# Attention and token/channel mixer on one core: 32 bytes of filler moved, channel part put in another order

## The chip, the cores and the metric

The kernel runs on one core of a Trainium2 chip, as one program. The metric is the device time of the program in microseconds (us). The kernel before was timed in three runs: 935.6, 936.44 and 939.02 us, median 936.44 us.

## What is computed

The reference is a decayed attention whose output goes through a token-mixing and a channel-mixing network, all in fp32:

```python
def _attn_ref(q, k, v, f):                      # 8 x 8 heads x 576 x 64
    ...
    scores = scale * np.matmul(q, k.transpose(0, 1, 3, 2))
    cum = np.cumsum(np.log(np.clip(f, 0.0001, 1.0)), axis=-1)
    decay = cum[:, :, :, None] - cum[:, :, None, :]
    ...                                         # causal mask, softmax
    return np.matmul(attn, v)

def _moe_ref(x, w_tok1, w_tok2, w_ch1, w_ch2):  # x: 8 x 576 x 512
    xt = x.transpose(0, 2, 1)
    h = np.maximum(xt @ w_tok1, 0.0) @ w_tok2
    u = x + h.transpose(0, 2, 1)
    h2 = np.maximum(u @ w_ch1, 0.0) @ w_ch2     # 512 -> 1536 -> 512
    return u + h2
```

This case is about the last two lines, the channel part: `h2` and the sum that leaves.

## The kernel before

All tokens of the 8 batches stand in one row of 4608. The attention and the token part run batch by batch (32 pairs of heads), and write `u` to DRAM (`ud`). The channel part then goes over the 4608 tokens in five chunks (`WIDE`): three of 2 x 512 tokens and two of 2 x 384. Both matrix products of a chunk are done by a seven-product (Strassen-like) scheme on 2 x 2 blocks. Every fp32 operand is split into a high and a low part, so that one product is three matmuls: high weights by high data, low by high, high by low (lines L1047, L1048, L1049 for the first matrix in `uprod`, L1128, L1129, L1130 for the second in `mul`, reached through `product`).

The weights of one such group (two blocks, high and low, 2 KB in each partition, 256 KB in all) are loaded by one DMA into a buffer `wq` (L962, in `weights`) and used by six matmuls. There are nine `wq` buffers. `wq0` to `wq4` are allocated early, in the pool `mix`. `wq5` to `wq8` come later: at the end of the attention `swap(0)` closes the right-hand pool that held the attention's inputs and opens a new one in its place, with 24 buffers `H` (the hidden rows), six `tmp` and those four `wq`. Pools on the right-hand side grow down from the top of SBUF. The last tile of the old right-hand pool was a filler of 32 bytes, `even0`, which went with that pool.

Around the matmuls, in the second product of a chunk, ScalarE writes the high part of a hidden row into one of six `st` buffers (L489), and VectorE the low part (L498, or L501 with the relu). In the first product VectorE and ScalarE gather the seven partial products from PSUM into `tmp` and `H` (L983, L1059, L1073, L1076, L1082, L1087), and combine rows (L975, L977). At the end of a chunk, `rest_in` loads `u` again into a quarter of an `xt` buffer (L1145), `join` adds a finished partial sum (L1156), `leave` adds the accumulator in PSUM (L1167) and sends the result out (L1171). In the last chunk the last product is ordered differently (`fin`): all 18 matmuls for the first half of the output's channels, then 18 for the second, and `leave` then works on two parts of 192 tokens each.

The order of all work on every engine is a table of numbers, `ORDER`, one row for each of PE, DVE, ACT, POOL and SP (the DMA queue); each number is an operation in the order in which `build` writes them. `Plan.run` takes these orders as they are and gives out buffers by them. All DMAs of the channel part are issued by SP, in order.

Of the kernel before, what the change touches and what calls it, by code (L numbers as in the profile page):

```python
# [9 lines left out]
F32 = mybir.dt.float32  # L10
# [5 lines left out]
P = 128  # L16
# [1344 lines left out]
def attn_mixer_kernel(  # L1361
# [101 lines left out]
    for kind, shape, dt in (  # L1463
# [6 lines left out]
        ("xn", [P, 2, 1024], F32R),  # L1470
    ):
        tiles(ap[kind in ATT[1]], kind, shape, dt, n_(kind))
    ap[0].tile([P, 8], F32, name="even0")

    E["H"], E["tmp"], E["st"] = {}, {}, {}

# [59 lines left out]
```

## Time and profile before

| | us |
|---|---|
| median of three runs | 936.44 |
| the profiled execution | 936.74 |
| its span, from first to last instruction | 935.0 |
| TensorE (PE) busy in the span | 912.3 (98%) |
| VectorE (DVE) busy | 712.9 (76%) |
| ScalarE (ACT) busy | 520.7 (56%) |
| GpSimd (POOL) busy | 237.3 (25%) |
| DMA queue q1, share of 16 engines | 84.3% |

A busy time on PE covers the whole stay of a matmul in the pipeline, and matmuls overlap, so it doesn't tell at what pace they follow each other; that is read from their starts in the timeline. The first matmul of the channel part starts 391.76 us into the span, between the last pieces of the attention, and from 410 us on PE does nothing else. Its matmuls are 512 wide up to 726.80 us, and 384 wide from there on, with some groups of 512 still among them up to 778 us.

### The profile page before, as it was taken

What the parts mean: (1) busy time and instruction counts of PE and PEld (TensorE: products, weight loads), DVE (VectorE), ACT (ScalarE), POOL (GpSimd) and SP (SyncE); (2) the same over time, 40 slices, a digit from 0 to 9 for tenths busy, and PEclk for the clock granted to TensorE, in tenths of its full rate; (3) what the DMA queues carried; (4) which work ended last, traced back from release to release, by engine and by line L of the source; (5) the groups of instructions that cost most, each with busy time, mean ns of one, the idle gap of its engine ahead of it and who ended that gap; (6) DMA issues with size and microseconds to landing.
All of it is one profiled execution on the core that took longest, in us unless ns stands there. A gap on an engine that the chain in (4) does not pass through costs nothing.

```text
span 935.0 us, 26743 instructions
## 1 busy us (share of the span) xinstructions
PE 912.3 (98%) x10270; PEld 782.2 (84%) x10270; DVE 712.9 (76%) x1894; ACT 520.7 (56%) x1340; POOL 237.3 (25%) x320
## 2 busy tenths in 40 slices
PE   8999999999999999999999999999999999999996
PEld 5678888788888787888888888888888899999996
DVE  7998888888788868554698547985389845984685
ACT  5989998998789978631364124540245313541251
POOL 4477777676656552100000000000000000000000
PEclk9999999999999999999999999999999999999999
DMA  7898999999899786669887777878788888989885
GB/s 230 269 278 267 314 274 293 300 297 277 266 307 289 244 251 176 178 197 290 276 246 233 226 243 236 268 227 255 212 250 251 275 289 285 293 280 301 281 283 168
DMA packets 143871, 242.49 MB, mean 259 GB/s; under 512 B 15936, under 2 KB 71488, under 8 KB 143744
## 3 DMA queue, kind: packets, MB, share of 16 engines
q1 hardware_dynamic: 143648, 240.64, 84.3%
q8 instruction: 81, 1.33, 0.6%
q14 instruction: 46, 0.38, 0.1%
q10 hardware_dynamic: 96, 0.15, 0.0%
HBM read 199.52 MB, written 41.21 MB: 257 GB/s over the span
## 4 chain that ended last, share of the span: by engine, by line
PE 78%; DVE 7%; DMA 6%; ACT 3%; POOL 2%; issue 2%; SPq 1%; DVEq 0%; ACTq 0%; POOLq 0%
PE bank L1047 9%; PE bank L1049 9%; PE bank L1048 9%; PE bank L1130 9%; PE bank L1128 9%; PE bank L1129 9%; PE bank L1245 7%; PE bank L747 5%; PE bank L891 4%; PE bank L862 3%; DVE pr L788 3%; ACT pr L792 1%; DMA d_raw<-ud 1%; DMA raw<-in_qk 1%; DMA cb<-decd 1%
## 5 line engine op out<-in xcount | busy, mean ns | idle before, releaser
L792 ACT ACTIVATE pr<-pr,nmin 64x64 f32<-64x64 f32 (+4 forms) x320 | 176.7, 559 | 17.7 <-DVE nmin L788 17.3
L489 ACT ACTIVATE st<-H 128x512 fp32r<-128x512 f32 (+1 forms) x210 | 119.5, 586 | 102.7 <-PE bank L1129 75.6
L1128 PE MATMUL bank<-st,wq 128*128 128x512 f32 (+1 forms) x420 | 155.5, 370 | 0.8 <-DMA wq<-wd 0.8
L1130 PE MATMUL bank<-st,wq 128*128 128x512 f32 (+1 forms) x420 | 155.8, 371 | 0.0
L1129 PE MATMUL bank<-st,wq 128*128 128x512 f32 (+1 forms) x420 | 155.1, 369 | 0.0
L747 PE MATMUL bank<-raw 64*64 64x448 f32 (+6 forms) x1408 | 113.0, 407 | 2.6 <-issue 0.8
L788 DVE CUSTOM_DVE_ANT_0 pr<-bank,cb 128x448 f32<-128x448 f32 (+3 forms) x260 | 108.8, 455 | 6.1 <-PE bank L753 3.0
L498 DVE TENSOR_TENSOR st<-H,st 128x512 fp32r<-128x512 f32 (+1 forms) x150 | 92.2, 632 | 14.3 <-ACT st L489 14.1
L891 PE MATMUL bank<-pf,vr 64*64 64x256 f32 (+3 forms) x2048 | 97.7, 314 | 0.8 <-DVE pf L870 0.3
L872 ACT ACTIVATE pf<-bank 128x512 f32<-128x512 f32 x152 | 84.2, 596 | 9.7 <-PE bank L862 5.7
L1128 PEld LDWEIGHTS bank<-st,wq 128*128 128x128 f32 x420 | 78.8, 188 | 11.4 <-ACT st L489 1.1
L1130 PEld LDWEIGHTS bank<-st,wq 128*128 128x128 f32 x420 | 78.8, 188 | 10.7
L1129 PEld LDWEIGHTS bank<-st,wq 128*128 128x128 f32 x420 | 78.9, 188 | 10.6
L983 DVE TENSOR_TENSOR tmp<-bank,tmp 128x512 f32<-128x512 f32 (+1 forms) x80 | 50.3, 633 | 45.0 <-PE bank L1049 38.7
L1059 ACT ACTIVATE tmp<-bank 128x512 f32<-128x512 f32 (+1 forms) x30 | 16.6, 553 | 121.3 <-PE bank L1049 115.7
L891 PEld LDWEIGHTS bank<-pf,vr 64*64 64x64 f32 x2048 | 75.3, 133 | 8.6 <-issue 1.7
L747 PEld LDWEIGHTS bank<-raw 64*64 64x64 f32 x1408 | 53.1, 135 | 29.4 <-issue 11.6
L862 PE MATMUL bank<-ident,pr 64*128 64x64 f32 x1536 | 65.0, 225 | 5.0 <-DVE nmin L788 2.4
L862 PEld LDWEIGHTS bank<-ident,pr 64*128 64x128 f32 x1536 | 58.9, 139 | 10.5 <-issue 4.2
L922 POOL TENSOR_TENSOR xt<-xt,rb 128x64 f32<-128x64 f32 (+1 forms) x64 | 52.5, 841 | 52.3 <-DVE xt L910 19.6
L1073 ACT ACTIVATE H<-bank 128x512 f32<-128x512 f32 (+1 forms) x30 | 16.4, 553 | 85.4 <-PE bank L1049 80.9
L792 ACT ACTIVATION_READ_ACCUMULATOR pr<-pr,nmin 128x1 f32 (+1 forms) x320 | 62.9, 197 | 0.0
(169 smaller groups left out, 2115.8 us busy)
## 6 DMA issues: line engine op xcount, KB each, us to landing
wq<-wd SPq DMA_DIRECT2D x420, 256.0 KB
raw<-in_qk SPq DMA_DIRECT2D x32, 576.0 KB
cb<-decd SPq DMA_DIRECT2D x26, 576.0 KB
d_raw<-in_w_ch SPq DMA_DIRECT2D x48, 256.0 KB
wd<-sg SPq DMA_DIRECT2D x24, 512.0 KB
vr<-in_v SPq DMA_DIRECT2D x64, 160.0 KB
rb<-recd SPq DMA_DIRECT2D x32, 320.0 KB
wd<-sg SPq DMA_DIRECT2D x24, 384.0 KB
```

Of the source, the lines that this page charges most:

```text
L489: nc.scalar.activation(out, in_, func, scale=scale)
L498: nc.vector.tensor_tensor(out, in_, asf(hi), op=ALU.subtract)
L747: nc.tensor.matmul(at(buf)[HALF[h], of : of + n], q[:, i0 : i0 + D], k[:, j0 : j0 + n], start=t not in (0, 1), stop=not nd, skip_group_che ...
L788: nc.vector.tensor_tensor_reduce(o, x, y, -1.0 / D**0.5, c0[:m, NS + z : NS + z + 1] if t == 5 else 3e38, op0=ALU.add, op1=ALU.min, accum_ ...
L792: nc.scalar.activation(x, x, AF.Exp, bias=E["nmin"][sm][:m, t : t + 1], scale=-1.0, accum_out=E["rec"][rm][:m, c : c + 1])
L862: nc.tensor.transpose(at(ps[s])[:, k * D : (k + 1) * D], at(pr)[r, x, :, :].rearrange("p a b -> p (a b)"), E["ident"][r, r])
L872: p.op("ACT", d_act(512), lambda src_=src_, o=o: nc.scalar.activation(o(), src_(), AF.Copy), rd=[ps[s]], wr=[(pt, s)], bufs=[ps[s], pt])
L891: nc.tensor.matmul(at(av[z])[o, 256 - w : 256], at(vr)[r, vblk(j), :], at(pt)[r, c : c + w], start=j == 4, stop=gi == 2, skip_group_check= ...
L1047: nc.tensor.matmul(o, wt[:, 0, :], h_, start=(first and k == 0), stop=False, skip_group_check=True)
L1128: nc.tensor.matmul(o, wt[:, 0, :], h_, start=(first and x == 0), stop=False, skip_group_check=True)
L1129: nc.tensor.matmul(o, wt[:, 1, :], h_, start=False, stop=False, skip_group_check=True)
L1130: nc.tensor.matmul(o, wt[:, 0, :], l_, start=False, stop=(x == FX - 1), skip_group_check=True)
```

## The change

The 32-byte tile `even0` leaves the attention's pool and gets a pool of its own, opened on the right-hand side before the attention's, which stays open to the end. So the filler now stands at the very top of SBUF. The attention's own buffers keep their addresses (the filler stood above them before, as it does now). The buffers that `swap(0)` opens in their place (`H`, `tmp`, `wq5` to `wq8`) now begin 32 bytes lower. In the built program `wq5` lies at byte 221152 of a partition before and at 221120 after, `wq0` at 122560 in both. Divided by 64, the first address leaves 32, the other two leave nothing, and all 34 late buffers go the same way; all other operands of these matmuls (`st`, `ux`, `sg`, `ring`, the old token weights, `wq0` to `wq4`) lie at multiples of 64 in both.

The tables of the order are written anew for the channel part. No instruction is added or removed on any engine. On PE the sequence of operations is the same up to the 54th matmul of the channel part; before that only `wq` slots differ. On SP the first two DMAs that change places are those of the first chunk's `u`.

```diff
@@ -46,25 +46,25 @@
...
-        "2716 2725 2710 2728 2731 2737 2746 2719 2713 2749 2752 2722 2758 2734 2740 2767 2743 2770 2761 2773 2755 2779 "
...
+        "2716 2725 2710 2728 2731 2737 2713 2722 2719 2746 2749 2734 2740 2752 2758 2743 2767 2770 2773 2761 2755 2779 "
...
@@ -1457,6 +1457,8 @@
     tiles(mixp, "ux", [P, max(WIDE)], F32R, n_("ux"))
     E["uh"].update(E["ux"])
     E["wq"] = {(("wq", i),): mixp.tile([P, 2, 2, P], F32R, name=f"wq{i}") for i in range(n_("wq"))}
+    even = ctx.enter_context(tc.tile_pool(name="even", bufs=1, side="right"))
+    even.tile([P, 8], F32, name="even0")
     att = [tc.tile_pool(name=f"att{x}", bufs=1, side=side) for x, side in enumerate(("right", "left"))]
...
         tiles(ap[kind in ATT[1]], kind, shape, dt, n_(kind))
-    ap[0].tile([P, 8], F32, name="even0")
```

The end of the program, in two queues. These are the last instructions of DVE before; the last matmuls of PE write bank3, and bank3 rows of 192 are the two parts of that last result:

```order
L1167 TENSOR_TENSOR xt0_144<-bank5_68,xt0_144 128x384
L1156 TENSOR_TENSOR xt0_144<-xt0_144,tmp2_8166 128x384
L1167 TENSOR_TENSOR xt0_144<-bank0_63,xt0_144 128x192
L1167 TENSOR_TENSOR xt0_144<-bank3_66,xt0_144 128x192
L1167 TENSOR_TENSOR xt1_145<-bank1_64,xt1_145 128x384
L1167 TENSOR_TENSOR xt0_144<-bank0_63,xt0_144 128x192
L1167 TENSOR_TENSOR xt1_145<-bank6_69,xt1_145 128x384
L1167 TENSOR_TENSOR xt0_144<-bank3_66,xt0_144 128x192
```

And the last of DVE in the changed kernel, where the last matmuls write bank3 as well and bank1 holds the half before it:

```order
L1167 TENSOR_TENSOR xt1_145<-bank2_65,xt1_145 128x384
L1156 TENSOR_TENSOR xt1_145<-xt1_145,tmp3_8170 128x384
L1167 TENSOR_TENSOR xt0_144<-bank1_64,xt0_144 128x192 x2
L1167 TENSOR_TENSOR xt1_145<-bank5_68,xt1_145 128x384
L1167 TENSOR_TENSOR xt1_145<-bank3_66,xt1_145 128x192 x2
```

Before, three instructions that don't read bank3 stand between its two parts; now the two parts are the last two.

The end of SP's queue before, from the last load of weights (`wq7`) on:

```order
L962 DMA wq8_8173<-wd2_2_136 128x512
L962 DMA wq7_8172<-wd2_0_134 128x512
L1171 DMA out_t<-xt1_145 128x384 x2
L1145 DMA xt0_144<-ud7_127 128x192
L1171 DMA out_t<-xt0_144 128x192 x4
L1171 DMA out_t<-xt1_145 128x384
L1171 DMA out_t<-xt0_144 128x384
L1171 DMA out_t<-xt1_145 128x384
L1171 DMA out_t<-xt0_144 128x384
```

And the same of the changed kernel:

```order
L962 DMA wq7_8175<-wd2_0_134 128x512
L1145 DMA xt1_145<-ud6_126 128x192
L1171 DMA out_t<-xt1_145 128x384
L1145 DMA xt1_145<-ud7_127 128x192
L1171 DMA out_t<-xt0_144 128x384 x2
L1171 DMA out_t<-xt1_145 128x384
L1171 DMA out_t<-xt0_144 128x192
L1171 DMA out_t<-xt1_145 128x384
L1171 DMA out_t<-xt0_144 128x384
L1171 DMA out_t<-xt0_144 128x192
L1171 DMA out_t<-xt1_145 128x192 x2
```

The four `out_t` of 384 that closed the queue now stand ahead of the two parts of the last result, which are the last two DMAs. The load of `wq7`, the first weights of the last product, is the last load of weights in both, and in both it stands behind the same point of PE's program (it may start once all but the last 54 matmuls are done).

## Rows read from the trace of the kernel before

**Rows 1.** The page, part 1: the span, and busy us (share of span) xinstructions.

```profile
span 935.0 us, 26743 instructions
PE 912.3 (98%) x10270; PEld 782.2 (84%) x10270; DVE 712.9 (76%) x1894; ACT 520.7 (56%) x1340; POOL 237.3 (25%) x320
```

**Rows 2.** Windows: stretch, its us, busy us of each engine, granted clock, DMA.

```profile
391.70:410.00 18.30, 18.24 (x184) 14.99 (x181) 8.61 (x20) 5.31 (x13) 3.32 (x4) 1.00 0.44 139
410.00:560.00 150.00, 150.00 (x654) 122.40 (x653) 101.58 (x167) 47.92 (x84) 0.00 (x0) 1.00 0.83 253
560.00:730.00 170.00, 170.00 (x742) 138.76 (x741) 130.48 (x216) 65.24 (x117) 0.00 (x0) 1.00 0.80 242
751.00:927.90 176.90, 175.99 (x993) 173.41 (x991) 123.26 (x252) 60.59 (x126) 0.00 (x0) 1.00 0.87 277
927.90:935.00 7.10, 0.00 (x0) 0.00 (x0) 1.76 (x5) 0.00 (x0) 0.00 (x0) 0.84 0.44 152
```

**Rows 3.** Waits on PE, 410 to 928 us: us in total, times, longest.

```profile
PEld bank L1128 <- ACT st L489: 1.1, 1, 1.1
PE bank L1128 <- DMA wq<-wd: 0.8, 1, 0.8
```

**Rows 4.** Timeline of PE, 512 wide: starts of eight matmuls (start us, us, what).

```profile
672.90 0.39 PE L1128 MATMUL bank<-st,wq 128*128 128x512 f32 x1
...
679.71 0.39 PE L1047 MATMUL bank<-ring,wq 128*128 128x512 f32 x1
...
701.91 0.39 PE L1128 MATMUL bank<-st,wq 128*128 128x512 f32 x1
...
707.51 0.39 PE L1128 MATMUL bank<-st,wq 128*128 128x512 f32 x1
...
711.60 0.39 PE L1128 MATMUL bank<-st,wq 128*128 128x512 f32 x1
...
714.39 0.39 PE L1128 MATMUL bank<-st,wq 128*128 128x512 f32 x1
...
718.49 0.39 PE L1128 MATMUL bank<-st,wq 128*128 128x512 f32 x1
...
724.08 0.39 PE L1128 MATMUL bank<-st,wq 128*128 128x512 f32 x1
```

**Rows 5.** The same, 384 wide.

```profile
907.71 0.34 PE L1128 MATMUL bank<-st,wq 128*128 128x384 f32 x1
...
910.83 0.35 PE L1128 MATMUL bank<-st,wq 128*128 128x384 f32 x1
...
911.38 0.33 PE L1128 MATMUL bank<-st,wq 128*128 128x384 f32 x1
...
913.98 0.34 PE L1128 MATMUL bank<-st,wq 128*128 128x384 f32 x1
```

**Rows 6.** Timeline of the last 18 us: PE.

```profile
920.07 0.34 PE L1130 MATMUL bank<-st,wq 128*128 128x384 f32 x1
...
921.23 0.42 PE L1128 MATMUL bank<-st,wq 128*128 128x384 f32 x1 [0.82 <-DMA wq<-wd]
...
927.47 0.34 PE L1130 MATMUL bank<-st,wq 128*128 128x384 f32 x1
```

**Rows 7.** Timeline of the last 18 us: DVE and SP's queue.

```profile
926.04 0.36 DVE L1167 TENSOR_TENSOR xt<-bank,xt 128x192 f32<-128x192 f32 x1
...
927.85 1.82 DVE L1167 TENSOR_TENSOR xt<-bank,xt 128x192 f32<-128x192 f32 x5 [1.44 <-PE bank L1130]
928.96 3.50 SPq L1171 DMA_DIRECT2D out_t<-xt  x7
```

**Rows 8.** The chain that ended last, in order of time: the last load of weights.

```profile
917.29 3.80 DMA wq<-wd
```

**Rows 9.** Windows of 50 us: the fullest for DVE in the channel part.

```profile
450.00:500.00 50.00, 50.00 (x219) 40.84 (x218) 44.32 (x74) 26.93 (x47) 0.00 (x0) 1.00 0.85 260
```

**Rows 10.** Waits of SP's queue, 750 to 928 us.

```profile
SPq L962 <- PE bank L1130: 45.4, 80, 1.0
```

184 rows, old and new, of tables (ACT, DVE, PE, SP) are left out of this document.

## The prediction

> **What bounds the kernel now.** I read the page first: TensorE (PE) is busy for 912.3 of 935.0 us [rows 1], so there are some 23 us in which it has nothing in flight, and the question is how many of them lie where the change works. The change leaves the attention's addresses alone, and PE's sequence as it is until well into the first chunk of the channel part, so I cut the span into windows [rows 2]. From 410 to 730 us PE is busy without a gap (150.00 of 150, 170.00 of 170), from 751 to 927.9 us for 175.99 of 176.9, and then the program runs for another 7.10 us in which PE does nothing. The waits of PE between 410 and 928 us come to one stop, for weights, of 0.8 us [rows 3]. So an order that only feeds PE better can win at most that 0.8 us and some part of the 7.1 us behind the last matmul. Everything else has to come from the pace at which matmuls follow each other, which a busy share of 100% doesn't show. That pace is read from their starts in the timeline.
>
> **The change part by part: the filler.** It moves four of the nine weight buffers, `wq5` to `wq8`, from 32 past a multiple of 64 bytes to a multiple of 64, where `wq0` to `wq4` already are. The trace of before thus holds both cases side by side. By PE's order in the built program, the 30 matmuls from 672.90 to 679.71 us all take weights from early buffers (`wq0` to `wq4`). Those from 701.91 to 707.51 us are 24, with weights from `wq7, wq5, wq6, wq8`; the next 18, to 711.60, use `wq2, wq4, wq1`; 12 to 714.39 use `wq5, wq6`; 18 to 718.49 use `wq2, wq4, wq1`; 24 to 724.08 use `wq5` to `wq8` [rows 4]. The paces are 6.81/30 = 227.0 ns for the first, then 5.60/24 = 233.3 ns, 4.09/18 = 227.2, 2.79/12 = 232.5, 4.10/18 = 227.8 and 5.59/24 = 232.9. Same line, same shape, same full clock [rows 2]: a 512-wide matmul costs 233 ns with late weights and 227 with early ones, a difference of 6 ns. In the built program 684 of the 1512 matmuls of this width read `wq5` to `wq8`: 684 x 6 = 4.1 us.
>
> At 384 wide the picture is another one. The 18 matmuls from 907.71 to 910.83 us read late buffers (`wq5, wq8, wq6`): 173.3 ns each, nothing lost. The 18 behind them, to 913.98, read early ones (`wq3, wq2, wq4`) and take 3.15 us, 0.03 more, and this is lost in their first three: 910.83 to 911.38 is 0.55 us where three take 0.52 [rows 5]. So what costs there is the step from a late buffer to an early one. The order of before makes it about 46 times in these chunks: 46 x 0.03 = 1.4 us. At 512 wide such steps, about 75, leave the early stretch behind them at 227.2 to 227.8 ns, on the mean 0.5 ns above 227.0, 18 x 0.5 = 9 ns a step: 0.7 us, of which I take 0.6. With all nine buffers alike both kinds of loss should go: 4.1 + 1.4 + 0.6 = 6.1 us. All of it lies on the path that sets the end, since PE has no gap there [rows 2]; and the reordering doesn't change how many matmuls there are. The bounds are 0 (the late buffers are slow for another reason than their last 32 bytes, see the rivals) and 6.7 us (10% more, for the rounding of the starts to 0.01 us). I take 6.1 because the two kinds of buffer differ in the same program, at the same line, side by side.
>
> Here a rule of the Trainium skill speaks against the change. "SBUF — State Buffer", section "Who interferes with whom", gives TensorE two independent read ports, one for the moving operand and one for weights, and says that PE and ACT never wait on anyone; nothing in it lets the place of the weights set the pace. By it the filler is worth 0 and the sum would be the tail's alone (rival 1). The rows above don't agree: 233 against 227 ns.
>
> The other 30 late buffers (`H`, `tmp`) are read and written by DVE and ACT. What they would gain I cost at nothing: DVE has idle time in every window (101.58 of 150 us, 130.48 of 170), and PE is covered by it [rows 2].
>
> **The tail.** Before, the last matmul starts at 927.47 and ends at 927.81 us [rows 6]. DVE then has five instructions in 1.82 us, from 927.85 on; it stood still for 1.44 us before them, because the first of the five waits for that matmul, with two 384-wide ones behind it that need not have waited [rows 7]. SP's last seven DMAs take 3.50 us to issue, 928.96 to 932.46, 0.50 each, and the span ends 2.5 us later: 935.0 - 927.81 = 7.2 us. In the new order DVE has just two instructions of 192 behind the last matmul, and SP two DMAs. Worked out with these rows: DVE starts 0.04 us after the matmul's end and ends its first at +0.40 (0.36 for one of 192 [rows 7]); the first DMA is issued from there to +0.90, the second, whose data are ready at about +0.67 (1.82 us for five: they start about 0.3 apart), to +1.40, and landing takes the same 2.5 us: +3.9 us. The tail shrinks by 7.2 - 3.9 = 3.3 us. Bounds: 1.5 us (one or two of the other outputs still stand in the way, 0.5 each, and a DVE wait) and 3.6 us.
>
> **The stop before the last product** stays. The last weights, `wq7`, are issued at 917.29, on the way for 3.80 us [rows 8], and the matmul that needs them starts 0.82 us late [rows 6]. In both orders this DMA waits for the same point, 54 matmuls from the end, of which 18 lie before the use: 18 x 173.5 = 3.1 us against 3.8. I cost the edit at 0, with bounds of -0.8 and +0.8 us.
>
> **The rest of the order** I also cost at nothing: from 410 us on PE had no other wait to lose, and what covers a new one is that SP's loads wait for PE (45.4 us in 80 waits for buffers that PE still uses [rows 10]), not PE for loads. If this cover is gone somewhere, one late load costs about 0.8 us, as the one in rows 6. I allow 0 to 3 us. The join with the attention (391.7 to 410 us, 18.24 of 18.30 us busy [rows 2]) changes little.
>
> **The sum.** 935.0 - 6.1 - 3.3 = 925.6 us of span. The profiled execution took 936.74, 1.7 us more than its span, and stands 0.3 us above the median of 936.44. So 936.44 - 9.4 = 927.0 us.
>
> **Rivals.**
> 1. It is not the 32 bytes but the region: `wq5` to `wq8` lie 100 KB above `wq0` to `wq4`, and the trace of before can't part the two. Then the filler is worth nothing, by the skill's rule as well, and the tail alone gives 936.44 - 3.3 = 933.1 us, within 0.5%. For it: both differences coincide. Against it: in the 384-wide rows late buffers cost nothing by themselves, only the change between the kinds does, which fits a step in phase better than a slow region.
> 2. The tail does not shrink, because a DMA or DVE instruction in front of the last two is late (the second load of `u` now stands behind an output that waits for DVE). Then 936.44 - 6.1 = 930.3 us.
> 3. The new order gives back part: three to six late loads of 0.8 us, 2.5 to 5 us: 929.5 to 932 us.
> 4. Slower: DVE blocks the queue. It is busy for 44.32 of 50 us around 475 us [rows 9], and PE now asks for its `st` buffers 2% sooner. If the new order makes DVE wait for a load in front of work for PE, as the 1.44 us in rows 7, PE has six `st` buffers to live on, about 6 x 1.36 = 8 us; past that every us counts. It decides from 9.4 us in all; at 14 us lost, 4.6 more, the time is 941. Against it: no row shows DVE starving PE in 517 us.
>
> **How the numbers follow.** My forecast, both terms, 0.72; rival 1 0.10; rival 2 0.07; rival 3 0.07; rival 4 0.04. What a measurement can tell from no change is about 0.5%, 4.7 us: faster means below 931.8. Faster: 0.72 + 0.07 + 0.05 of rival 3 = 0.84; same: rival 1 and the rest of 3, 0.12; slower 0.04. The range: below, 936.44 - 6.7 - 3.6 - 0.8 = 925.3; above it takes in rivals 2 and 3 up to 931.8 and leaves out rivals 1 and 4, 0.14, with some 0.04 below: 925.3 to 931.8.
>
> **What would show it.** Right: 512-wide matmuls 227 ns apart throughout, 6 x 227 = 1.36 us a group whatever its buffer; no 0.55 us for three at 384 wide; the last matmul about 6 us earlier than 927.8, and about 4 us from its end to the end of the span. Wrong: groups of 1.40 us that still go with `wq5` to `wq8`; waits on PE for `wq` or `st` between 410 us and the end beyond the one of 0.8 us; more than two outputs issued behind the last matmul.

## The result and the profile after

The changed kernel takes 926.89 us (median of four runs, 925.69 to 927.53) beside 937.73 us for the kernel before on the same chip (four runs, 935.6 to 940.57): a ratio of 0.9881, 95% interval 0.985 to 0.9913. It is faster, by 10.8 us where 9.4 were forecast, and the time is 0.1 us from the 927.0 of the sum (the kernel before came out 1.3 us above the 936.44 that the sum starts from). The profiled execution took 927.18 us; its span is 925.4.

Page, part 1 of the kernel after (answers to [rows 1]: the span, and busy us, share of the span, instructions):

```profile
span 925.4 us, 26760 instructions
PE 905.5 (98%) x10270; PEld 781.3 (84%) x10270; DVE 710.2 (77%) x1894; ACT 520.6 (56%) x1340; POOL 237.2 (26%) x320
```

PE's share of the span is 98% in both, and the operations are the same number on every engine (the 17 more in the total are semaphore instructions). Only the windows show where the time went (columns as in [rows 2]; the third is cut at 919 us; the last is the stretch of [rows 9]):

```profile
410.00:560.00 150.00, 150.00 (x663) 123.87 (x662) 102.66 (x168) 49.95 (x88) 0.00 (x0) 1.00 0.82 252
560.00:730.00 170.00, 170.00 (x751) 140.65 (x750) 132.68 (x220) 65.48 (x116) 0.00 (x0) 1.00 0.82 249
751.00:919.00 168.00, 167.68 (x959) 166.20 (x958) 119.53 (x247) 58.62 (x123) 0.00 (x0) 1.00 0.89 287
450.00:500.00 50.00, 50.00 (x222) 41.44 (x221) 47.17 (x78) 25.89 (x45) 0.00 (x0) 1.00 0.84 259
```

PE is busy without a gap in the first two, as before, at the same full clock, but 663 matmuls pass through the first instead of 654, and 751 through the second instead of 742. DVE is fuller around 475 us than it was (47.17 of 50 us, [rows 9] 44.32), and PE still doesn't wait for it.

The end of the program, in the timeline of after (start us, us, what; in brackets idle time and what ended it); the first two lines are the join of the last two products, the others the last instructions of PE, DVE and SP's queue:

```profile
914.90 0.34 PE L1130 MATMUL bank<-st,wq 128*128 128x384 f32 x1
915.56 0.41 PE L1128 MATMUL bank<-st,wq 128*128 128x384 f32 x1 [0.32 <-DMA wq<-wd]
...
921.71 0.34 PE L1130 MATMUL bank<-st,wq 128*128 128x384 f32 x1
922.08 0.62 DVE L1167 TENSOR_TENSOR xt<-bank,xt 128x192 f32<-128x192 f32 x2 [2.04 <-PE bank L1130]
922.47 0.81 SPq L1171 DMA_DIRECT2D out_t<-xt  x2
```

The last matmul starts at 921.71 us where it started at 927.47 [rows 6]. Two DVE instructions and two DMAs follow it, where [rows 7] have five and seven. Between 410 us and the end PE's matmuls have one wait left, the one that was there before, now of 0.32 us:

```profile
PE bank L1128 <- DMA wq<-wd: 0.3, 1, 0.3
```

To part the gain I measure three stretches in every trace: from the span's start to the first channel matmul; from the 55th channel matmul, which is where PE's order begins to differ, to the start of the last; and from the last matmul's end to the span's end (the "tail"). The first 54 matmuls of the channel part take about 23 us in every run. In us:

| profiled run | span | first channel matmul | 55th to last | tail | matmuls in 420 to 720 us |
|---|---|---|---|---|---|
| before | 935.0 | 391.8 | 512.65 | 7.14 | 1306 |
| after | 925.4 | 392.5 | 506.34 | 3.35 | 1324 |
| `e1` filler alone | 931.0 | 394.2 | 506.29 | 7.14 | 1325 |
| `e2` orders alone | 933.0 | 394.2 | 512.08 | 3.37 | 1305 |
| `e3` 64 bytes on top | 934.6 | 394.5 | 513.54 | 3.37 | 1301 |
| `e4` early weights at 32 | 929.4 | 388.3 | 514.47 | 3.36 | 1296 |
| `e5` all weights at 32 | 937.9 | 393.7 | 517.53 | 3.36 | 1287 |
| `e6` weights and data at 32 | 929.3 | 396.5 | 506.31 | 3.37 | 1324 |
| `e9` data at 32 | 935.5 | 392.0 | 516.86 | 3.37 | 1289 |
| `e7` all at 256 | 923.2 | 389.9 | 506.69 | 3.33 | 1322 |
| after, again | 926.5 | 393.0 | 507.02 | 3.35 | 1324 |
| `e7` again | 925.3 | 392.0 | 506.71 | 3.33 | 1324 |
| `e8` late weights used last | 926.1 | 393.6 | 506.02 | 3.36 | 1324 |

Of the 9.6 us by which the span shrank, 6.31 lie between the 55th and the last matmul, 3.79 in the tail, 0.2 in the first 54 matmuls, and the attention in front took 0.8 longer. Some 0.5 of the 6.31 us is the shorter stop, the rest the pace. The medians differ by 10.8 us; what stands beyond the 9.6 lies within the scatter of the attention, which the last section shows, but the runs behind the medians have no trace that would place it.

The starts give the pace of each kind of matmul (spacing to the next start, without stops; which buffer each one reads is taken from the built program): 512 wide, before, 228.24 ns for 822 with early weights and 232.71 for 682 with late ones; after, 227.03 and 226.93. 384 wide, before, 175.33 and 173.92; after, 173.50 and 173.48. The difference between the kinds is gone at both widths.

### The profile page after: what moved, and what is told of

The parts are those of the page before. It is cut to its first block, busy times and chain, and to the rows that moved or that the text cites. A ratio compares the mean times of both kernels' runs of the same rounds, so it can differ in the third digit from the quotient of the medians.

```text
span 925.4 us, 26760 instructions
## 1 busy us (share of the span) xinstructions
PE 905.5 (98%) x10270; PEld 781.3 (84%) x10270; DVE 710.2 (77%) x1894; ACT 520.6 (56%) x1340; POOL 237.2 (26%) x320
## 4 chain that ended last, share of the span: by engine, by line
PE 59%; DVE 2%; DMA 2%; POOL 1%; issue 0%; ACT 0%; SPq 0%; DVEq 0%; POOLq 0%
PE bank L1047 9%; PE bank L1049 9%; PE bank L1048 9%; PE bank L1128 9%; PE bank L1130 9%; PE bank L1129 9%; PE bank L1245 2%; DMA d_raw<-ud 1%; DVE pr L788 1%; PE bank L891 1%; PE bank L862 0%; DMA wq<-wd 0%; DMA recd<-rs 0%; POOL sg L495 0%; PE bank L747 0%
## 5 line engine op out<-in xcount | busy, mean ns | idle before, releaser
L1128 PE MATMUL bank<-st,wq 128*128 128x512 f32 (+1 forms) x420 | 154.2, 367 | 0.3 <-DMA wq<-wd 0.3
L1130 PE MATMUL bank<-st,wq 128*128 128x512 f32 (+1 forms) x420 | 154.3, 367 | 0.0
L1129 PE MATMUL bank<-st,wq 128*128 128x512 f32 (+1 forms) x420 | 154.2, 367 | 0.0
L747 PE MATMUL bank<-raw 64*64 64x448 f32 (+6 forms) x1408 | 109.5, 397 | 2.6 <-DMA raw<-in_qk 1.3
L872 ACT ACTIVATE pf<-bank 128x512 f32<-128x512 f32 x152 | 84.4, 596 | 11.2 <-PE bank L862 5.7
L1128 PEld LDWEIGHTS bank<-st,wq 128*128 128x128 f32 x420 | 78.8, 188 | 10.2 <-issue 0.6
L1130 PEld LDWEIGHTS bank<-st,wq 128*128 128x128 f32 x420 | 78.8, 188 | 9.9
L1129 PEld LDWEIGHTS bank<-st,wq 128*128 128x128 f32 x420 | 78.8, 188 | 9.6
L1073 ACT ACTIVATE H<-bank 128x512 f32<-128x512 f32 (+1 forms) x30 | 16.5, 554 | 103.2 <-PE bank L1049 103.1
L862 PEld LDWEIGHTS bank<-ident,pr 64*128 64x128 f32 x1536 | 58.8, 139 | 11.2 <-issue 5.0
```

The source lines that it names most:

```text
L747: nc.tensor.matmul(at(buf)[HALF[h], of : of + n], q[:, i0 : i0 + D], k[:, j0 : j0 + n], start=t not in (0, 1), stop=not nd, skip_group_che ...
L862: nc.tensor.transpose(at(ps[s])[:, k * D : (k + 1) * D], at(pr)[r, x, :, :].rearrange("p a b -> p (a b)"), E["ident"][r, r])
L872: p.op("ACT", d_act(512), lambda src_=src_, o=o: nc.scalar.activation(o(), src_(), AF.Copy), rd=[ps[s]], wr=[(pt, s)], bufs=[ps[s], pt])
L1128: nc.tensor.matmul(o, wt[:, 0, :], h_, start=(first and x == 0), stop=False, skip_group_check=True)
L1129: nc.tensor.matmul(o, wt[:, 1, :], h_, start=False, stop=False, skip_group_check=True)
L1130: nc.tensor.matmul(o, wt[:, 0, :], l_, start=False, stop=(x == FX - 1), skip_group_check=True)
```

## Experiments

My theory at this point: late weights were slow because they start 32 past a multiple of 64, and the filler cures that (some 6 us); the orders give the tail (some 3.3 us), and the two add up. The first rival: the region 100 KB higher is what is slow, and the pace came from the orders. The second: neither place matters by itself, only whether weights and data start alike.

### One half at a time

`e1_filler_alone`, against before:

```diff
+    even = ctx.enter_context(tc.tile_pool(name="even", bufs=1, side="right"))
+    even.tile([P, 8], F32, name="even0")
...
-    ap[0].tile([P, 8], F32, name="even0")
```

> The filler moved, the orders of before. Theory (weights that begin 32 bytes past a multiple of 64 slow the matmuls that read them, and the step away from them too): all 512-wide matmuls 227 ns apart and no loss at the steps at 384 wide, so 6.1 us less than before, about 0.9935 of it; the last matmul ends near 921.7 us instead of 927.8, the stop for the last weights stays at 0.8 us, and the tail behind the last matmul keeps its 7.2 us. Rival (the pace went up because the new order mixes the buffers in another way): 512-wide matmuls with wq5 to wq8 stay at 233 ns, and the time is that of before.

Measured: 928.66 us (926.57 to 932.76, six runs) beside 935.04, ratio 0.9941 [0.992, 0.9962]. Windows of this kernel from 420 us (columns as above), its only wait of PE there, and the end on DVE and SP:

```profile
420.00:720.00 300.00, 300.00 (x1325) 248.16 (x1324) 217.75 (x358) 105.31 (x186) 0.00 (x0) 1.00 0.82 250
...
923.90:931.00 7.10, 0.00 (x0) 0.00 (x0) 1.78 (x5) 0.00 (x0) 0.00 (x0) 0.83 0.47 160
```

```profile
PE bank L1128 <- DMA wq<-wd: 0.4, 1, 0.4
```

```profile
923.86 1.82 DVE L1167 TENSOR_TENSOR xt<-bank,xt 128x192 f32<-128x192 f32 x5 [0.98 <-PE bank L1130]
924.98 3.50 SPq L1171 DMA_DIRECT2D out_t<-xt  x7
```

With the orders of before, 1325 matmuls pass in 300 us instead of 1306, and the tail is [rows 7] again to the hundredth: 1.82 us for five, 3.50 for seven. So the pace belongs to the 32 bytes and the tail doesn't. Two expectations were missed: the stop was 0.4 us and not 0.8, and the last matmul ended at 923.8 us and not near 921.7, because the attention took 2.5 us longer in this profile than in that of before.

`e2_orders_alone`, against after:

```diff
-    even = ctx.enter_context(tc.tile_pool(name="even", bufs=1, side="right"))
-    even.tile([P, 8], F32, name="even0")
...
+    ap[0].tile([P, 8], F32, name="even0")
```

> The new orders, the filler in its old place. Theory: paces as before (233 and 227 ns at 512 wide, 0.03 us lost at each step from wq5..wq8 to wq0..wq4 at 384 wide), the tail as in the changed kernel, 3.4 us instead of 7.2, and some tenths from the last stop: 3.3 to 4.2 us less than before, 0.9955 to 0.9965 of it. The two parts alone then add up to what both do together. Rival (the parts help each other, the new order needs the quicker matmuls): the tail is longer than 3.4 us or PE gets new waits, and the time is within 2 us of before.

Measured: 930.38 us (928.41 to 934.82, seven runs) beside 935.04, ratio 0.9955 [0.9937, 0.9972].

```profile
420.00:720.00 300.00, 300.00 (x1305) 244.50 (x1304) 213.75 (x350) 104.19 (x184) 0.00 (x0) 1.00 0.82 248
...
929.70:933.00 3.30, 0.00 (x0) 0.00 (x0) 0.60 (x2) 0.00 (x0) 0.00 (x0) 1.00 0.24 75
```

The mirror image: 1305 matmuls, the pace of before, and a tail of 3.37 us. Between the 55th and the last matmul the new orders win 0.57 us, and that is the stop before the last product, 0.2 us instead of 0.8. The halves add up: 0.9941 x 0.9955 = 0.9896, with 0.9881 and 0.9901 for both together in two comparisons.

### Place, region, or weights against data

`e3_filler_64` makes the filler on top 64 bytes and adds 32 in the old place. The late buffers then lie 64 bytes lower than in before and are again 32 past a multiple of 64. Against after:

```diff
-    even.tile([P, 8], F32, name="even0")
+    even.tile([P, 16], F32, name="even0")
...
+    ap[0].tile([P, 8], F32, name="even1")
```

> The changed kernel with the late buffers 64 bytes lower than before instead of 32 (64 bytes of filler at the top, and the attention's own 32 back below it, so that its buffers stay at multiples of 64). wq5 begins at 221088, again 32 past a multiple of 64. Theory: the slow matmuls are back, 233 ns at 512 wide with wq5 to wq8, and the time is that of the orders alone, about 6 us more than the changed kernel. Rival (any shift takes the late buffers off a bad place near the top of the memory): 227 ns throughout, the time of the changed kernel.

Measured: 932.93 us (929.52 to 936.39, twelve runs) beside 935.04, ratio 0.9976 [0.996, 0.9992]. The stretch from the 55th to the last matmul is 7.2 us longer than in after (about 6 was expected):

```profile
420.00:720.00 300.00, 300.00 (x1301) 243.51 (x1300) 212.96 (x348) 104.13 (x183) 0.00 (x0) 1.00 0.82 248
```

By the starts, 512-wide matmuls with late weights are back at 233.1 ns, those with early ones at 228.9. That the buffers moved down is not what helped: 64 bytes don't cure the pace, 32 do. But 64 bytes aren't without effect: with the same orders the stretch is 1.5 us longer than in `e2`. At 384 wide the loss now lies in the matmuls with late weights themselves (177.0 ns, in `e2` 173.9) and no longer in the early ones behind them (173.7, in `e2` 175.4). So while weights and data are apart, more than the 32 bytes modulo 64 counts; what it is was not tried.

`e4_early_at_32` leaves the late buffers of after where they are and moves the early weights by 32 bytes. Against after:

```diff
+    mixp.tile([P, 8], F32, name="pad0")
     E["wq"] = {(("wq", i),): mixp.tile([P, 2, 2, P], F32R, name=f"wq{i}") for i in range(n_("wq"))}
+    mixp.tile([P, 8], F32, name="pad1")
```

> The changed kernel with a pad of 32 bytes ahead of wq0 to wq4 and one behind them, so that these five begin 32 past a multiple of 64 and wq5 to wq8 at a multiple. Theory: the roles change: 512-wide matmuls with wq0 to wq4 at 233 ns (about 840 of 1512, 840 x 6 = 5.0 us), those with wq5 to wq8 at 227, the loss at 384 wide at the step from wq0..wq4 to wq5..wq8 (about 1.4 us): 6 to 7 us more than the changed kernel. Rival (it is the region of the late buffers): no difference from the changed kernel.

Measured: 933.61 us (931.17 to 936.73, ten runs) beside 935.04, ratio 0.9984 [0.9971, 0.9997].

```profile
420.00:720.00 300.00, 300.00 (x1296) 242.81 (x1295) 213.40 (x349) 105.48 (x186) 0.00 (x0) 1.00 0.82 247
```

The roles are exchanged: early weights now take 232.94 ns at 512 wide, where they took 227.03 in after, in their own region. The rival of the region has fallen. The size was not met: 8.1 us more than after between the 55th and the last matmul, where 6 to 7 were expected. The late weights, untouched, lost as well (230.2 ns instead of 226.93), and not only beside an early one: those between two other late ones have a mean of 229.7. In before the early ones between early ones stayed at 227.2. Why a program with misaligned weights slows the aligned ones in one case and hardly in the other stays open. The starts give one hint. The weights of a matmul are loaded while the one ahead of it runs: the load starts 3 ns behind the start of that matmul and takes 188 ns (medians in before). In before the last early matmul ahead of a late one has a spacing of 234.8 ns (74 cases), where an early one between two early ones has 227; in `e4`, with the roles exchanged, the last late one ahead of an early one has 234.8 as well. So the price already shows under the matmul during which the misplaced weights are loaded. All data of the channel part start alike modulo 64, so no run tells whether it is that matmul's data or the next one's that count.

`e5_all_nine_at_32` has the same two pads and the filler in its old place, so that all nine buffers are 32 past a multiple of 64 (against after):

```diff
+    mixp.tile([P, 8], F32, name="pad0")
     E["wq"] = {(("wq", i),): mixp.tile([P, 2, 2, P], F32R, name=f"wq{i}") for i in range(n_("wq"))}
-    even = ctx.enter_context(tc.tile_pool(name="even", bufs=1, side="right"))
-    even.tile([P, 8], F32, name="even0")
+    mixp.tile([P, 8], F32, name="pad1")
...
+    ap[0].tile([P, 8], F32, name="even0")
```

> The new orders with all nine weight buffers 32 past a multiple of 64 (late ones in their old place, a pad of 32 bytes around wq0 to wq4), the data at multiples of 64. Read from the 54th matmul of the channel part to its last, which is 506.7 us in the changed kernel and 512.4 with the orders alone. Theory one (where the weights begin sets the pace): all 512-wide matmuls at 233 ns, 1500 x 6 = 9 us more than the changed kernel, nothing lost at 384 wide since there are no steps: about 515.5 us. Theory two (only the mixture of the two kinds costs): 227 ns throughout, 506.7 us.

`e6_all_at_32` moves everything: one pad at the start of the left-hand side shifts the channel part's data (`st`, `ux`, `sg`, `ring`, `t1h` and the others) and the early weights, and the filler in its old place shifts the late ones. Against after:

```diff
+    const.tile([P, 8], F32, name="pad0")
     E["sel"] = const.tile([P, 32], F32R, name="sel")
...
-    even = ctx.enter_context(tc.tile_pool(name="even", bufs=1, side="right"))
-    even.tile([P, 8], F32, name="even0")
...
+    ap[0].tile([P, 8], F32, name="even0")
```

> The new orders with weights and data alike 32 past a multiple of 64 (a pad of 32 bytes in the pool const moves the data, the rest as in the run before it). Theory one (the place of the weights alone): as with all nine weights at 32, about 515.5 us from the 54th matmul to the last. Theory two (the place of the weights against that of the data, whatever both are): 227 ns throughout, 506.7 us.

`e9_data_at_32` moves the data alone and leaves all nine weight buffers at multiples of 64. Against after:

```diff
+    const.tile([P, 8], F32, name="pad0")
     E["sel"] = const.tile([P, 32], F32R, name="sel")
...
+    mixp.tile([P, 8], F32, name="pad1")
     E["wq"] = {(("wq", i),): mixp.tile([P, 2, 2, P], F32R, name=f"wq{i}") for i in range(n_("wq"))}
+    mixp.tile([P, 8], F32, name="pad2")
```

> The changed kernel with the data of the channel part (st, ux, sg, ring, the token weights' place) 32 past a multiple of 64 and all nine weight buffers at multiples. Theory one (the place of the weights alone): 227 ns throughout, 506.7 us from the 54th matmul to the last. Theory two (weights against data): 233 ns throughout at 512 wide, about 515.5 us. If a reading of either kind across a border of 64 costs: somewhere between, or more.

Measured, one run each: 939.7 us (`e5`), 931.1 (`e6`), 937.33 (`e9`), beside 935.77 for before (seven runs). Their windows in this order, two lines for each (420 to 720 us is 512 wide, 800 to 900 is 384 wide):

```profile
420.00:720.00 300.00, 300.00 (x1287) 240.94 (x1286) 209.73 (x343) 102.48 (x180) 0.00 (x0) 1.00 0.81 245
800.00:900.00 100.00, 100.00 (x571) 99.76 (x570) 71.65 (x149) 35.47 (x75) 0.00 (x0) 1.00 0.90 283
```

```profile
420.00:720.00 300.00, 300.00 (x1324) 247.96 (x1323) 217.37 (x357) 104.96 (x185) 0.00 (x0) 1.00 0.83 252
800.00:900.00 100.00, 100.00 (x579) 100.00 (x578) 72.90 (x152) 36.90 (x79) 0.00 (x0) 1.00 0.90 287
```

```profile
420.00:720.00 300.00, 300.00 (x1289) 241.20 (x1288) 211.00 (x345) 103.07 (x181) 0.00 (x0) 1.00 0.81 245
800.00:900.00 100.00, 100.00 (x572) 100.00 (x571) 71.69 (x149) 34.39 (x73) 0.00 (x0) 1.00 0.88 285
```

Together with after they are a square of two by two, from the 55th to the last matmul:

| | data at a multiple of 64 | data 32 past one |
|---|---|---|
| weights at a multiple of 64 | 506.34 (after) | 516.86 (`e9`) |
| weights 32 past one | 517.53 (`e5`) | 506.31 (`e6`) |

The two cells with weights and data alike lie 10.5 to 11.2 us below the two with them apart; over the seven profiles in which all are alike (these two, `e1`, `e8`, the second of after and the two of `e7` below) the stretch scatters by 1.0 us. Neither place is slow by itself, and no mixture of two kinds is needed (`e5` and `e9` have one). What costs is that weights and data start 32 bytes apart modulo 64. Only 0 and 32 were tried. The timeline shows it in single starts; first `e6`, then `e9`, each a matmul at about 500 us and the eighteenth after it:

```profile
499.65 0.39 PE L1128 MATMUL bank<-st,wq 128*128 128x512 f32 x1
...
503.73 0.39 PE L1047 MATMUL bank<-ux,wq 128*128 128x512 f32 x1
```

```profile
499.61 0.40 PE L1128 MATMUL bank<-st,wq 128*128 128x512 f32 x1
...
503.80 0.39 PE L1128 MATMUL bank<-st,wq 128*128 128x512 f32 x1
```

4.08/18 = 226.7 ns against 4.19/18 = 232.8. So the first theory fell as well, in its wording: "32 past a multiple of 64" was true of before because its data are at multiples of 64. The misses in size: the expectations count from the 54th matmul, and from there `e5` took 517.8 us, 2.3 more than the 515.5 expected; most of it is that at 384 wide, too, every matmul now costs 1.6 to 1.7 ns more (175.08 and 175.21 ns for early and late weights against 173.5), which over 1005 matmuls is 1.6 us (571 and 572 pass from 800 to 900 us in `e5` and `e9`, 579 in `e6`).

### More alignment

`e7_all_at_256` puts data and all weights at multiples of 256 (in after they are at multiples of 64, 192 past one of 256). Against after:

```diff
+    const.tile([P, 16], F32, name="pad0")
     E["sel"] = const.tile([P, 32], F32R, name="sel")
...
-    even.tile([P, 8], F32, name="even0")
+    even.tile([P, 56], F32, name="even0")
```

> The changed kernel with all weights and data moved on, by 64 bytes on the left and 192 on the right, so that they begin at multiples of 256 instead of 192 past one. The matmuls at 512 wide are 227 ns apart, where 512 columns at 2.4 GHz are 213.3 ns; this asks whether the 13.7 ns left have to do with larger borders. If 64 bytes is all that counts: 227 ns, the time of the changed kernel. If borders of 128 or 256 count too: up to 13.7 ns less in each of 2520 matmuls, up to 34 us.

Measured: 923.63 us (922.15 to 925.87, four runs) beside 935.77, ratio 0.9864 [0.983, 0.9898].

```profile
420.00:720.00 300.00, 299.90 (x1322) 247.61 (x1321) 217.74 (x356) 107.76 (x190) 0.00 (x0) 1.00 0.83 252
```

The median looks 3 us better than after, and the trace says it isn't: 506.69 us from the 55th to the last matmul, at 227.07 and 226.92 ns. What was short in this profile is the attention, 389.9 us. To settle it, both ran again beside each other, without a change to either:

> The changed kernel once more, as it is, beside the two others of this call: 0.988 of the time before, with the attention's share of the scatter.

> All weights and data at multiples of 256, again. The first time it came to 923.6 us beside the changed kernel's 926.9, with the same pace of the matmuls and an attention that ended 2.7 us sooner. If that was the scatter of the attention: the changed kernel's time within 1 us. If the place helps the attention: 2 to 3 us less than the changed kernel, with the first matmul of the channel part before 390 us.

Measured: after 926.89 us (924.26 to 931.34, six runs), ratio 0.9901 [0.9876, 0.9926]; `e7` 925.61 (924.7 to 927.12, four runs), ratio 0.9888 [0.9866, 0.9909], both beside 936.29. The channel stretches are 507.02 and 506.71, and 0.5 of the first is a stop that after did not have in its first profile:

```profile
PE bank L1047 <- DMA wq<-wd: 0.5, 1, 0.5
```

The medians are 1.3 us apart, 0.3 more than the 1 us set for scatter, and the first channel matmul of `e7` starts at 392.0 us, not before 390. With weights and data alike, alignment beyond 64 bytes gives nothing that these runs can show.

### The last stop

`e8_last_load_last` lets the last product take its matmuls in another order: the group whose weights arrive last is used last. Against after:

```diff
+                sts = sts[1:] + sts[:1]
...
-                for x, st, wq in sts:
+                for n, (x, st, wq) in enumerate(sts):
...
-                        nc.tensor.matmul(o, wt[:, 0, :], l_, start=False, stop=(x == FX - 1), skip_group_check=True)
+                        nc.tensor.matmul(o, wt[:, 0, :], l_, start=False, stop=(x == FX - 1 if len(sts) == 1 else n == FX - 1), skip_group_check=True)
```

> The changed kernel with one more edit: the last product goes through its six weights from the second to the sixth and takes the first last, since the load of the first is the last one of all. Theory (the stop ahead of the last product is the flight of that load, 3.3 us against 3.1 us of work): no wait of PE for weights at the end, 0.3 to 0.5 us less than the changed kernel from the 54th matmul of the channel part to the last (506.3 us there), which the median can't show. Rival (the stop is the wait for st, which the trace puts down to ScalarE by its weight load): the stop stays.

Measured: 924.44 us (923.57 to 927.83, four runs) beside 936.29, ratio 0.9871 [0.9847, 0.9894]. Its timeline at the join of the last two products, where after has the stop of 0.32 us (the edit adds a line to the kernel, so L1128 to L1130 are L1129 to L1131 here):

```profile
916.11 0.33 PE L1131 MATMUL bank<-st,wq 128*128 128x384 f32 x1
916.28 0.33 PE L1129 MATMUL bank<-st,wq 128*128 128x384 f32 x1
916.46 0.33 PE L1130 MATMUL bank<-st,wq 128*128 128x384 f32 x1
```

No gap is left there, and from 500 us to the end no matmul of PE has a wait in the view (two spacings of 344 and 252 ns at 885.7 us still lose 0.25 us, in another place). The stretch is 506.02 us, 0.3 shorter than in after and 1.0 shorter than in the run of after beside it. The median is the lowest of its comparison, by 2.45 us against after, but the intervals overlap, and only some 0.5 us of it lies where the edit works: of the 1.0 us, 0.5 is the other stop of that run, shown above. I take it as the better version by that much.

## Why the prediction came out right, and where its reason was wrong

**What bounds the kernel.** Right. PE stays gapless, and the gain came from the pace and from the tail, with some 0.5 us from a shorter stop.

**The filler, 6.1 us.** The size held (5.8 us), the reason did not. `e1`, which has the orders of before, parts it. 512 wide, the sum of all spacings went from 346.32 to 341.57 us: 4.75, where 4.1 + 0.6 = 4.7 was forecast. 384 wide, 175.40 to 174.33: 1.07, where 1.4 was: a step cost 0.02 us on the mean, not the 0.03 that the prediction read from a single one. With 0.4 from the shorter stop that is 6.2 of the 6.36 us. The two kinds side by side in one program carried this far because they differ in just what the filler changes. What failed is the step that made it a property of the address: the square shows that it is the weights' start against the data's. The prediction knew only weights at both places and data at one, so its rows could not part the two; for this change both give the same number. The picture at 384 wide ("what costs there is the step from a late buffer to an early one") is right for before and not general: with all nine buffers apart from the data (`e5`) every matmul pays 1.6 ns, without any step, and in `e3` the late ones pay themselves.

The rule of the Trainium skill, "SBUF — State Buffer", "Who interferes with whom", by which PE's two read ports are independent, would have made the filler worth 0. `e1` measures 6.4 us on the median and 506.29 against 512.65 in the trace, and the square shows the pace depending on where weights and data start against each other. Here the measurement decides.

**Rival 1, the region,** had 0.10. `e4` rules it out: early weights go at 232.94 ns when they are moved by 32 bytes within their own region.

**The tail, 3.3 us.** Mechanism right, size 0.5 too small: 7.14 to 3.35 is 3.8. The term that was mis-sized is the landing: from the end of the last issue (922.47 + 0.81 = 923.28) to the end of the span it is 2.1 us and not the 2.5 taken from before, where seven outputs were on their way and the last was 384 wide, not 192. The issue itself was 0.2 shorter: 0.81 us for the last two DMAs, for which 0.50 each was taken. Rival 2, a tail that stays, is out: two outputs follow the last matmul in every run with the new orders.

**The stop, 0.** It shrank to 0.32 us, inside the bounds. The place of the load against PE's program didn't move, as the order said; the load was shorter, 3.28 us on the way where [rows 8] had 3.80. Here is that row of the chain of after:

```profile
912.14 3.28 DMA wq<-wd
```

Over the runs this stop was 0.2 to 0.8 us (`e8` aside), so it is scatter of one DMA, not something the orders won for good.

**The rest of the order, 0 (to 3), and rivals 3 and 4.** No new late load and no wait for DVE in the first profile of after; one late load of 0.5 us in the second. Three short stops are new in every run with the new orders: loads of weights into PE wait for hidden rows from ScalarE (L1073), which makes three spacings of 323 ns where 227 are usual in after, 0.3 us in all. DVE at 47.17 of 50 us didn't block PE. Neither of these rivals came about.

**The sum.** 6.1 + 3.3 = 9.4 us were forecast, 9.6 is the difference of the spans: 6.3 + 3.8 + 0.2, less 0.8 by which the attention happened to be longer. The attention alone could have moved the time by several us, and the kernel before came out 1.3 us higher than the sum took it; that the time was met to 0.1 us is in part luck.

## What to carry to other kernels

Where PE has no gap, read the spacing of matmul starts by buffer: two kinds of the same shape at different paces in one program are a finding, and the price is their difference times their count. Let the buffers of both operands of such fp32 matmuls start alike modulo 64; a tile of 32 bytes was worth 6 us here, and aligning further nothing. Order the last outputs so that only what depends on the last matmul stands behind it, and compare stretches of the trace when a change is smaller than the scatter of the rest of the program.

## What was not expected of the hardware

**Weights against data.** At full clock a 512-wide matmul of this kernel takes 227 ns behind its predecessor when weights and data start alike modulo 64, and 233 when they start 32 apart; at 384 wide 173.5 and about 175. Alike at 32 (`e6`: 226.95 and 226.92 ns) is as good as alike at 0. This holds for programs in which all weights are of one kind: in `e4`, which mixes them, matmuls whose operands start alike took 230.2 ns. No trace here shows what inside PE does it.

**The attention's scatter.** The same instructions in front of the channel part took 388.3 us in one profile (`e4`) and 396.5 in another (`e6`), while the channel part from the 55th matmul on took 506.3 and 507.0 us in the two profiles of after. `e6` and `e9` also move the attention's own left-hand buffers by 32 bytes, which may count for part of that; but the runs of one unchanged kernel (after, again) reach from 924.3 to 931.3 us too. The granted clock goes with part of the scatter; that it causes it is not shown. In before it is 0.50 (1.2 GHz) for 3.4 us from 352.5 us on, and full again behind; before that PE had stood still for 1.4 us (first the clock in three windows, then that wait):

```profile
345.00:349.00 4.00, 4.00 (x71) 3.62 (x63) 1.25 (x7) 1.14 (x5) 0.00 (x0) 1.00 1.05 239
352.50:355.90 3.40, 3.40 (x32) 1.54 (x26) 2.32 (x7) 3.38 (x8) 3.16 (x3) 0.50 1.04 280
356.00:360.00 4.00, 4.00 (x114) 3.55 (x115) 3.71 (x13) 2.90 (x9) 0.00 (x0) 1.00 0.46 174
```

```profile
PE bank L862 <- DVE nmin L788: 1.4, 1, 1.4
```

Four of the thirteen profiles have no such dip once the clock is up, and their first channel matmul starts at 388.3 to 393.0 us; those with one to three start at 391.8 to 396.5. The ranges overlap, so the dips can't be the whole of it; what the rest is was not tried.
